# Gate and value of the last eight units by 15 products over three feature blocks, three contraction blocks and two pairs of units

## The chip, the cores and the metric

The kernel runs on one core of one Trainium2 chip. Its time is the device time of one launch in microseconds, as the median of several runs. The engines are named as in the profile: PE is TensorE (PEld its weight loads), DVE is VectorE, ACT is ScalarE, POOL is GpSimd, SP is SyncE, which here only issues transfers. All data are fp32. A written matmul in fp32 appears as two TensorE instructions in the profile.

## The reference

An RWKV-5 attention over 768 tokens, 4 batches and 8 heads of width 48 is followed by a SwiGLU block on its 3072 output rows of width 384:

```python
for t in range(S):
    cur = einsum(u * k[t], v[t])
    y[t] = einsum(r[t], state + cur)
    state = w * state + einsum(k[t], v[t])
x = y as (3072, 384)
g = x @ w_gate                      # 384 x 1536
silu = g * (1.0 / (1.0 + np.exp(-g)))
out = (silu * (x @ w_val)) @ w_out  # 1536 x 384
```

## The kernel before, in words

**Tiling.** A tile of 128 tokens of one batch is a step `i`, 24 in all. Attention handles one step at a time, in chunks: `scores(i)` (key times query, masked into `At`), `outputs(i)` (the step's output, copied by ACT into `xT`, which holds ten steps), `update(i)` (the state `Z`). From step 12 on, keys and queries are turned by block: `scale_k` and `scale_r` on POOL write them into `hats`, `move_blocks` has SP issue 16 small copies of 32x32 blocks, and `turn_blocks` on DVE transposes within the blocks. A diagonal (`diagonal`, eight ACT operations) is written into `At` before `scores` adds the rest by a predicated copy.

The SwiGLU block works on units `g` of two steps, 256 tokens; there are 12. Width 384 is three contraction blocks of 128 (`CC`), the 1536 features are 12 blocks `f`. `wg` and `wv` hold the gate and value weights, `wo` the output weights. The hidden values of unit `g` are `hT[g]`, twelve blocks of 128 features by 256 tokens.

- Units 0 and 1: `gate_value(g, f)` makes six products per block and unit.
- Units 2 to 11 go in pairs (`four_units(g)` for g = 2, 4, 6, 8, 10). For each feature block the two pairs of operands (gate and value weights; units g and g+1) are multiplied with a seven-product scheme over two contraction blocks, and four plain products add the third: 11 products of 128x256 in place of 12. `w_sums` (POOL) makes sums of weights for two feature blocks at a time, `x_sums` (DVE) sums of inputs for a pair, and after each product ACT or DVE collects the accumulators `c_a` and `c_b` into `hT`. SiLU is a sigmoid on ACT (`sg`) and a product on DVE; the second unit's last product (`h1`) is on POOL.
- `project(g, n)`, n = 0 to 6, makes the output rows of a unit with seven groups of six products of 192 columns, with sums of hidden values from `h_sums` (DVE, tiles `hs`). `two_projections(g)` lists the 14 items of two units in the order "00 10 01 02 11 04 03 12 05 06 13 14 15 16" (unit, n), and hangs `h_sums`, `w_sums` and `x_sums` of the next pair on some of them.

**Order.** All engines run their instructions in the order written. A loop over `s` interleaves attention with SwiGLU work from the list `todo`: `gaps(s, n)` calls `feed`, which takes the next pieces; `queue(g)` puts a pair's pieces on the list when its units exist, and from s = 9 on each group of four steps shares them out evenly. After the loop, `feed(len(todo))` issues what is left and the last two units are projected. In `queue`, the first item of a pair's projections (`then`) is put ahead of the last piece of its `four_units`, and three pieces of the next `four_units` are put between the last items of a projection.

**Memory.** PSUM has four banks for attention (`ps_a`), one each in `ps_w` and `ps_o`, and two in `ps_f`. In SBUF, `hT` is a pool of two buffers, `w_bits` a ring of three (raw weights at first, then `s` and `hs`), `part` a ring of six, `w_low` of two.

Of the kernel before, what the change touches and what calls it, by code (L numbers as in the profile page):

```python
# [9 lines left out]
FP32 = mybir.dt.float32  # L10
INT32 = mybir.dt.int32
UINT32 = mybir.dt.uint32
AF = mybir.ActivationFunctionType
ALU = mybir.AluOpType
AX = mybir.AxisListType
P = 128
# [6 lines left out]
def fast(  # L23
# [25 lines left out]
    B, H, S, D = r.shape  # L49
    D2 = 2 * D  # L50
    VW = 2 * D + 16
    HP = H // 2
    R2 = 64 + D
    NCH = S // P
    N = B * NCH
    DM, DFF = moe_w_gate.shape
    CC, FC = DM // P, DFF // P
# [21 lines left out]
    ones = cst.tile([P, 1], FP32, name="ones")  # L79
    ident = cst.tile([P, P], FP32, name="ident")  # L80
    mask = cst.tile([P, P], FP32, name="mask")
    wg = cst.tile([P, CC, DFF], FP32, name="wg")
    wv = cst.tile([P, CC, DFF], FP32, name="wv")
    wo = cst.tile([P, FC, DM], FP32, name="wo")
    NX = 10
    xT = cst.tile([P, NX, CC, P], FP32, name="xT")
    Z = [cst.tile([P, HP, D2], FP32, name=f"Z{b}") for b in range(B)]
    r_ld = [cst.tile([P, H, D], FP32, name=f"r_ld{i}") for i in range(2)]
    k_ld = [cst.tile([P, H, D], FP32, name=f"k_ld{i}") for i in range(2)]
# [48 lines left out]
    NW = len(chunks)  # L138
# [131 lines left out]
        base=0, pattern=[[1, P]], channel_multiplier=-1,  # L270
    )
    dve.tensor_scalar(held[:], wcol[:], W_LOW, W_HIGH, ALU.max, ALU.min)
    tables = two.tile([P, 2, HP, P + 32], FP32, name="tables", tag="hT")
    pw, pv = tables[:, 0, :, 0 : P + 1], tables[:, 1, :, 0:P]
    dve.memset(pw[:, :, P : P + 1], 1.0)
    dve.tensor_copy(pw[:, :, P - 1 : P], held[:].unsqueeze(2))
    for l in range(7):
        n = 1 << l
# [158 lines left out]
                pool.tensor_mul(ze, ze, w)  # L437


    hT = {}  # L440

    def gate_value(g, f):
        if f == 0:
            hT[g] = two.tile([P, FC, 2 * P], FP32, name="hT", tag="hT")
        gv = ps_f.tile([P, 2, 2 * P], FP32, name="gv", tag="gv")
        for o, wt in enumerate((wg, wv)):
            for c in range(CC):
                pe.matmul(  # L448
                    gv[:, o, :].rearrange("p (i t) -> p i t", i=2),
                    wt[:, c, P * f : P * (f + 1)], xT[:, 2 * g % NX : 2 * g % NX + 2, c, :],  # L450
                    start=(c == 0), stop=(c == CC - 1),
                )
        sg = three.tile([P, 2 * P], FP32, name="sg", tag="sg")
        act.activation(sg[:], gv[:, 0, :], AF.Sigmoid)
        dve.tensor_mul(sg[:], sg[:], gv[:, 0, :])
        dve.tensor_mul(hT[g][:, f, :], sg[:], gv[:, 1, :])
# [101 lines left out]
    def x_halves(g):  # L558

        i = [2 * (g + j) % NX for j in range(2)]  # L560
        return [[xT[:, i[j] : i[j] + 2, c, :] for j in range(2)] for c in range(CC)]

    def x_sums(g):
        (x11, x12), (x21, x22), _ = x_halves(g)
        ta, tb = (two.tile([P, 2, 2, P], FP32, name=n, tag="w_low") for n in ("t12", "t34"))
        t1, t2, t3, t4 = ta[:, 0], ta[:, 1], tb[:, 0], tb[:, 1]
        dve.tensor_sub(t1, x12, x11)
        dve.tensor_sub(t2, x22, t1)
        dve.tensor_sub(t3, x22, x12)
        dve.tensor_sub(t4, x21, t2)  # L570
        part_of.setdefault(g, {})["t"] = (t1, t2, t3, t4)

    def w_sums(g, f):

        (w11, w12, w13), (w21, w22, w23) = (
            [w[:, c, P * f : P * (f + 2)] for c in range(CC)] for w in (wg, wv)
        )
        t = three.tile([P, 4, 2 * P], FP32, name="s", tag="w_bits")
        x = part_of.setdefault(g, {})
        x["s", f] = x["s", f + 1] = t  # L580
        if g == 2:
            pool.tensor_add(t[:, 0], w21, w22)
            pool.tensor_sub(w21, t[:, 0], w11)
        else:
            pool.tensor_add(t[:, 0], w21, w11)  # L585
        pool.tensor_sub(t[:, 1], w22, w21)
        pool.tensor_sub(t[:, 2], w12, w21)
        pool.tensor_sub(t[:, 3], w13, w23)

    def four(g, f, what):  # L590

        x = part_of[g]
        if what == "p1":
            if f == 0:
                for j in range(2):
                    hT[g + j] = two.tile([P, FC, 2 * P], FP32, name="hT", tag="hT")
            x["a", f] = ps_f.tile([P, 2, 2 * P], FP32, name="c_a", tag="gv")[:, 0]
        elif what == "p2":
            pool_of, tag = ((ps_o, "o"), (ps_w, "w_mag"))[f % 2]
            x["b", f] = pool_of.tile([P, 2 * P], FP32, name="c_b", tag=tag)[:]  # L600
        h = [hT[g + j][:, f, :] for j in range(2)]
        if what in ("sg0", "sg1"):
            j = int(what[2])
            x[what, f] = three.tile([P, 2 * P], FP32, name="sg", tag="sg")
            act.activation(x[what, f][:], h[j], AF.Sigmoid)  # L605
            return
        if what == "h1":
            dve.tensor_mul(h[1], h[1], x.pop(("sg1", f))[:])  # L608
            pool.tensor_mul(h[1], h[1], x.pop(("u3", f))[:])  # L609
            return  # L610
        (w11, w12, w13), (s2, w22, w23) = (
            [w[:, c, P * f : P * (f + 1)] for c in range(CC)] for w in (wg, wv)
        )
        (x11, _), (x21, x22), (x31, x32) = x_halves(g)
        s1, s3, s4, s5 = (x["s", f][:, n, P * (f % 2) : P * (f % 2 + 1)] for n in range(4))
        t1, t2, t3, t4 = x["t"]
        acc, lhs, rhs, first = {
            "p1": ("a", w11, x11, True), "p6": ("a", s2, t2, False), "p7": ("a", s3, t3, False),
            "p4": ("a", w22, t4, False), "c21": ("a", w23, x31, False),
            "p2": ("b", w12, x21, True), "c11": ("b", w13, x31, False),  # L620
            "p5": ("b", s1, t1, True), "c22": ("b", w23, x32, False),
            "p3": ("b", s4, x22, False), "c12": ("b", s5, x32, False),
        }[what]
        ps = x[acc, f]
        pe.matmul(  # L625
            ps.rearrange("p (i t) -> p i t", i=2), lhs, rhs,
            start=first, stop=what not in ("p2", "p5", "p4", "p3"), skip_group_check=True,
        )
        if what in ("p1", "p6", "p7"):
            nm = {"p1": "p1", "p6": "u2", "p7": "u3"}[what]  # L630
            x[nm, f] = six.tile([P, 2 * P], FP32, name=nm, tag="part")
            act.copy(x[nm, f][:], ps)  # L632
        elif what == "c11":
            dve.tensor_add(h[0], x.pop(("p1", f))[:], ps)  # L634
        elif what == "c21":
            dve.tensor_mul(h[0], h[0], x.pop(("sg0", f))[:])
            dve.tensor_mul(h[0], h[0], ps)  # L637
        elif what == "c22":
            dve.tensor_add(x["u3", f][:], x["u3", f][:], ps)  # L639
        elif what == "c12":  # L640
            dve.tensor_add(h[1], x.pop(("u2", f))[:], ps)  # L641
# [15 lines left out]
    def two_projections(g):  # L657

        def item(j, p):
            if (j, p) in ((1, 0), (0, 1)):  # L660
                h_sums(g, p)
            elif (j, p) in ((1, 1), (0, 3)):
                h_sums(g + 1, p // 3)
            elif (j, p) == (1, 2) and g + 2 < N // 2:
                w_sums(g + 2, 0)
            elif (j, p) == (0, 6) and g + 2 < N // 2:
                x_sums(g + 2)
            project(g + j, p)
        order = "00 10 01 02 11 04 03 12 05 06 13 14 15 16".split()
        return [lambda j=int(o[0]), p=int(o[1]): item(j, p) for o in order]  # L670


    summed = []
    todo = []
# [9 lines left out]
    def queue(g):  # L684
        if g == 0:
            todo.extend(
                (2 * f2 + 2 if j + f else 0, lambda j=j, f=f: gate_value(j, f))
                for f2 in range(FC // 2) for j in range(2) for f in (2 * f2, 2 * f2 + 1)
            )
        elif g % 2 and g > 1:  # L690
            first, *others = two_projections(g - 3)
            *pieces, last = four_units(g - 1)

            then = two_projections(g - 1)[0]

            for k in range(3):
                others.insert(len(others) - 3 + k, pieces.pop(0))
            pieces = ([first] if g == 3 else []) + others + pieces + [then, last]
            todo.extend((NW + 4, x) for x in pieces)
# [104 lines left out]
    for s in range(4, N + 2):  # L804
# [31 lines left out]
        if s - 2 >= 4:  # L836
            gaps(s, 3)
        gaps(s, 4)
        if s == 12:

            dve.tensor_tensor(bad[:], held[:], wcol[:], ALU.not_equal)
            dve.tensor_reduce(badc[:], bad[:], axis=AX.X, op=ALU.add)
            dve.memset(ones[:], 1.0)
            n_ps = ps_a.tile([P, HP, P], FP32, name="n_ps", tag="a")
            pe.matmul(n_ps[0:1, 0, 0:1], badc[:], ones[:], start=True, stop=True)
            act.copy(outside, n_ps[0:1, 0, 0:1])
    assert done["pool"] == NW
    feed(len(todo))
    for piece in two_projections(N // 2 - 2)[1:]:
        piece()  # L850


# [411 lines left out]
```

## Time and profile before

| what | value |
|---|---|
| runs | 626.18, 625.35, 626.19 us; median 626.18 |
| profiled execution, span of core 0 | 623.3 us, mean granted TensorE clock 0.999 |
| median of the runs less this span | 2.9 us |
| PE busy | 611.0 us, 5040 instructions |
| DVE, ACT, POOL busy | 358.6, 238.9, 296.9 us |
| last product ends | 618.0 us; then an addition of 0.35 us and the output transfer |

The profiled execution's own time is its span and what lies around it on the device; no total is listed for it, so sums are made against the span, and the 2.9 us stand for the rest. In the rows, a line such as L625 is a line of the kernel, followed by engine, operation, output and inputs, shapes and count; after the bar come busy time, mean of one and the idle time before. Matmuls overlap, so their mean is longer than the step from one to the next. Times within the trace count from the start of the span. L625 is the product of `four`, L519 that of `project`, L605 and L608 the sigmoid and product of SiLU, L585 to L588 `w_sums`, L302 `scale_r`.

### The profile page before, as it was taken

What the parts mean: (1) busy time and instruction counts of PE and PEld (TensorE: products, weight loads), DVE (VectorE), ACT (ScalarE), POOL (GpSimd) and SP (SyncE); (2) the same over time, 40 slices, a digit from 0 to 9 for tenths busy, and PEclk for the clock granted to TensorE, in tenths of its full rate; (3) what the DMA queues carried; (4) which work ended last, traced back from release to release, by engine and by line L of the source; (5) the groups of instructions that cost most, each with busy time, mean ns of one, the idle gap of its engine ahead of it and who ended that gap; (6) DMA issues with size and microseconds to landing.
All of it is one profiled execution on the core that took longest, in us unless ns stands there. A gap on an engine that the chain in (4) does not pass through costs nothing.

```text
span 623.3 us, 13014 instructions
## 1 busy us (share of the span) xinstructions
PE 611.0 (98%) x5040; PEld 552.1 (89%) x5040; DVE 358.6 (58%) x751; ACT 238.9 (38%) x647; POOL 296.9 (48%) x350
## 2 busy tenths in 40 slices
PE   8799999999999999999999999999999999999996
PEld 7688888899888899888899888899988899988896
DVE  6888997373566574466575355574354463355460
ACT  3368785312444412344331335422243321233310
POOL 4789789935556315364452636341334211443110
PEclk9999999999999999999999999999999999999999
DMA  7989873233232213322223312221000000000001
GB/s 187 218 215 252 260 242 65 50 62 82 57 60 34 40 16 76 65 42 46 44 34 70 78 16 32 31 41 38 26 1 2 2 0 26 26 1 2 1 2 56
DMA packets 138008, 40.47 MB, mean 65 GB/s; under 512 B 128592, under 2 KB 131792, under 8 KB 137936
## 3 DMA queue, kind: packets, MB, share of 16 engines
q1 hardware_dynamic: 134480, 34.82, 26.4%
q10 hardware_dynamic: 3456, 4.72, 2.1%
q8 instruction: 42, 0.69, 0.5%
q14 instruction: 30, 0.25, 0.1%
HBM read 28.51 MB, written 4.72 MB: 53 GB/s over the span
## 4 chain that ended last, share of the span: by engine, by line
PE 90%; POOL 2%; DMA 1%; ACT 1%; DVE 1%; issue 0%; SPq 0%; ACTq 0%; POOLq 0%
PE c_b L625 25%; PE c_a L625 21%; PE o_f L519 13%; PE o_a L519 8%; PE gv L448 7%; PE o_b L519 6%; PE y_ps L409 5%; PE s_ps L379 3%; PE u_ps L424 1%; PE tp L341 1%; DMA r_ld<-in_r_dram 1%; POOL wg L216 1%; POOL wv L216 1%; POOL rk L228 0%; POOL hats L299 0%
## 5 line engine op out<-in xcount | busy, mean ns | idle before, releaser
L609 POOL TENSOR_TENSOR hT<-hT,u 128x256 f32<-128x256 f32 x60 | 47.0, 785 | 148.7 <-DVE hT L608 121.6
L632 ACT COPY u<-c_a 128x256 f32<-128x256 f32 x120 | 44.5, 371 | 85.8 <-PE c_a L625 83.3
L625 PE MATMUL c_a<-t,wv 128*128 128x256 f32 x240 | 72.1, 382 | 0.1
L625 PE MATMUL c_b<-xT,wg 128*128 128x256 f32 x240 | 71.7, 380 | 0.0
L605 ACT ACTIVATE sg<-hT 128x256 f32<-128x256 f32 x120 | 50.0, 416 | 52.5 <-DVE hT L634 33.8
L320 ACT ACTIVATE At<-ident,du 128x128 f32<-128x128 f32 x176 | 62.0, 398 | 16.0 <-DVE o_sb L533 7.2
L625 PE MATMUL c_b<-xT,s 128*128 128x256 f32 x240 | 61.7, 380 | 0.0
L639 DVE TENSOR_TENSOR u<-u,c_b 128x256 f32<-128x256 f32 x60 | 25.1, 419 | 60.5 <-PE c_b L625 55.4
L625 PEld LDWEIGHTS c_a<-t,wv 128*128 128x128 f32 x240 | 45.0, 190 | 6.8 <-ACT u L632 1.2
L625 PEld LDWEIGHTS c_b<-xT,s 128*128 128x128 f32 x240 | 45.3, 190 | 6.5
L625 PEld LDWEIGHTS c_b<-xT,wg 128*128 128x128 f32 x240 | 45.4, 190 | 5.9
L634 DVE TENSOR_TENSOR hT<-p,c_b 128x256 f32<-128x256 f32 x60 | 25.2, 420 | 41.7 <-PE c_b L625 39.1
L585 POOL TENSOR_TENSOR s<-wv,wg 128x256 f32<-128x256 f32 x24 | 17.6, 734 | 65.5 <-PE o_f L519 50.8
L384 DVE COPY_PREDICATED At<-mask,s_ps 128x512 f32<-128x512 int32 x48 | 33.0, 741 | 21.3 <-PE s_ps L379 12.4
L302 POOL TENSOR_TENSOR hats<-r_ld,rscale 128x384 f32<-128x384 f32 x20 | 20.8, 1040 | 35.3 <-DMA hats<-hats 25.2
L448 PE MATMUL gv<-xT,wg 128*128 128x256 f32 x144 | 36.7, 391 | 0.6 <-ACT xT L413 0.6
L637 DVE TENSOR_TENSOR hT<-hT,c_a 128x256 f32<-128x256 f32 x60 | 25.3, 421 | 19.5 <-PE c_a L625 18.3
L641 DVE TENSOR_TENSOR hT<-u,c_b 128x256 f32<-128x256 f32 x60 | 25.2, 421 | 19.4 <-PE c_b L625 19.2
L625 PE MATMUL c_b<-t,s 128*128 128x256 f32 x120 | 36.2, 383 | 0.0
L409 PE MATMUL y_ps<-At,v_ld 128*32 128x128 f32 x768 | 34.9, 273 | 1.3 <-DVE At L384 1.3
L625 PE MATMUL c_b<-xT,wv 128*128 128x256 f32 x120 | 35.9, 381 | 0.0
L625 PE MATMUL c_a<-t,s 128*128 128x256 f32 x120 | 35.8, 380 | 0.0
(135 smaller groups left out, 1384.3 us busy)
## 6 DMA issues: line engine op xcount, KB each, us to landing
hats<-hats SPq DMA_DIRECT2D x192, 32.0 KB, 2.0
w_bits<-in_moe_w_gate_dram SPq DMA_DIRECT2D x6, 768.0 KB, 6.4
v_ld<-in_v_dram SPq DMA_DIRECT2D x48, 96.0 KB, 3.3
w_bits<-in_moe_w_val_dram SPq DMA_DIRECT2D x6, 768.0 KB, 6.3
w_bits<-in_moe_w_out_dram SPq DMA_DIRECT2D x6, 768.0 KB, 6.7
out_dram<-o_sb ACTq DMA_DIRECT2D x24, 192.0 KB, 1.9
k_ld<-in_k_dram SPq DMA_DIRECT2D x20, 192.0 KB, 3.1
r_ld<-in_r_dram SPq DMA_DIRECT2D x20, 192.0 KB, 3.8
```

The lines of the kernel that those rows point to most:

```text
L320: lambda h=h: act.activation(At[i % 2][:, h, :], ident[:], AF.Identity, scale=du[:, h : h + 1])
L384: dve.copy_predicated(At[i % 2][:].rearrange("p (a e) t -> p a e t", e=2)[:, :, e], mask[:].bitcast(INT32).unsqueeze(1).to_broadcast([P, H ...
L409: pe.matmul(ps[32 * q : 32 * q + 32, cc, :], *x, start=start, stop=stop, skip_group_check=True,)
L448: pe.matmul(gv[:, o, :].rearrange("p (i t) -> p i t", i=2), wt[:, c, P * f : P * (f + 1)], xT[:, 2 * g % NX : 2 * g % NX + 2, c, :], start ...
L519: pe.matmul(ps, lhs[:, f, :], rhs[:, f, :], start=(f == 0 and n in (0, 1, 4)), stop=(f == FH - 1), skip_group_check=True,)
L605: act.activation(x[what, f][:], h[j], AF.Sigmoid)
L609: pool.tensor_mul(h[1], h[1], x.pop(("u3", f))[:])
L625: pe.matmul(ps.rearrange("p (i t) -> p i t", i=2), lhs, rhs, start=first, stop=what not in ("p2", "p5", "p4", "p3"), skip_group_check=True,)
L632: act.copy(x[nm, f][:], ps)
L634: dve.tensor_add(h[0], x.pop(("p1", f))[:], ps)
L637: dve.tensor_mul(h[0], h[0], ps)
L641: dve.tensor_add(h[1], x.pop(("u2", f))[:], ps)
```

## The change

Units 0 to 7 keep their schemes. For units 8 to 11 `four_units` is replaced by `three_units(8)` and `three_units(10)`. A pair of units (512 tokens as two halves of 256) is worked through in four bands of three feature blocks. In each band a bilinear scheme of 15 products (r0 to r14) gives the 3 x 3 x 2 block product; each product is two matmuls, one for gate and one for value, into the two halves of one bank, so a band is 15 rounds of two matmuls of 128x256. The rounds go to seven accumulators: `n`, `y`, `l1`, `l5`, `l8` in attention's four banks in turn, `l4` in `ps_o`, `l2` in `ps_w`. Several rounds add to a bank after it was read once. ACT copies and DVE combinations collect them in `c`, six blocks of 128x512, and SiLU follows on operations of 512 columns: ACT, then DVE for two of a band's three feature blocks and POOL for one.

The weight operands: `in_place` (POOL, 24 operations, hung on the projections of units 6 and 7) overwrites three of nine weight blocks of a band for good; `w_forms` (POOL, nine operations a band) makes six more, in the ring or, for the first two bands of units 10 and 11, in memory of attention. `x_forms` (DVE, 11 operations a pair) makes the inputs' combinations. Buffers of attention hold `c`, the copies and the SiLU values: `hats`, `kT`, `At`, and `r_ld`, `k_ld`, `v_ld`, `Z` for operands.

`wg` and `wv` become the halves of one tile `wgv`, `hT` the halves of one tile `hTs`. `w_sums` no longer overwrites `w21` and makes five sums each time. The pieces of units 8 to 11 leave `todo`: after the loop the order is the first pair's bands, the projections of units 8 and 9 (the last two items between the first rounds of the next pair), the second pair's bands, and all items of units 10 and 11.

```diff
-        t = three.tile([P, 4, 2 * P], FP32, name="s", tag="w_bits")
+        t = three.tile([P, 5, 2 * P], FP32, name="s", tag="w_bits")
...
+        pool.tensor_add(t[:, 0], w21, w22)
+        pool.tensor_sub(t[:, 1], t[:, 0], w11)
+        pool.tensor_sub(t[:, 2], w22, t[:, 1])
+        pool.tensor_sub(t[:, 3], w12, t[:, 1])
+        pool.tensor_sub(t[:, 4], w13, w23)
...
+    THREES = 8
+    ROUNDS = (
+        ("r10", "n"), ("r14", "y"), ("r12", "l4"), ("r6", "l5"), ("r13", "n"), ("r2", "y"),
+        ("r9", "l4"), ("r3", "l1"), ("r5", "n"), ("r11", "y"), ("r7", "l5"), ("r1", "l2"),
+        ("r8", "l8"), ("r4", "l1"), ("r0", "l2"),
+    )
...
+    def prepare_threes(g, n):
+        if g == THREES:
+            if n in (0, 2, 4, 6):
+                in_place(n // 2)
+            if n == 7:
+                for do in w_forms(g, 0):
+                    do()
+        else:
+            if n == 10:
+                x_forms(g)
+            if n in (2, 6):
+                for do in w_forms(g, n // 4):
+                    do()
+
+    def three_step(g, t, n):
+
+        what, chain = ROUNDS[27 - n if t == 3 and n > 12 else n]
+        first = n == [c for _, c in ROUNDS].index(chain)
+        if first:
+            pool_of, tag = {"l4": (ps_o, "o"), "l2": (ps_w, "w_mag")}.get(chain, (ps_a, "a"))
+            wide[chain] = pool_of.tile([P, 2, 2 * P], FP32, name=f"c_{chain}", tag=tag)
+        u, v = wide["u", g, t][what], wide["v", g][what]
+        for o in range(2):
+            pe.matmul(
+                wide[chain][:, o].rearrange("p (i t) -> p i t", i=2), u[:, o], v,
+                start=first and o == 0, stop=True, skip_group_check=True,
+            )
...
+        for t in range(4):
+            z = 15 * t
+            for n in range(15):
+                todo.append((z + n, lambda t=t, n=n: three_step(g, t, n)))
+            if ("u", g, t + 1) not in wide and t < 3:
+                forms = w_forms(g, t + 1)
+                todo.append((z + 0.1, forms[0]))
+                todo += [(z + n + 0.2, do) for n, do in enumerate(forms[1:])]
+            later(z + 0.5, act.copy, q10, "n")
+            later(z + 1.5, act.copy, q14, "y")
+            later(z + 2.5, act.copy, r12, "l4")
+            later(z + 3.5, act.copy, r6, "l5")
+            later(z + 4.5, dve.tensor_add, q14, "n", q14)
+            later(z + 5.5, dve.tensor_add, q10, "y", q10)
+            later(z + 6.5, dve.tensor_sub, c[4], q14, "l4")
+            later(z + 8.5, act.copy, x, "n")
+            later(z + 9.5, act.copy, y, "y")
+            later(z + 9.6, pool.tensor_add, r6, y, r6)
+            later(z + 10.4, dve.tensor_add, c[2], y, "l1")
+            later(z + 10.5, dve.tensor_add, c[5], q10, "l5")
+            later(z + 11.5, dve.tensor_add, r12, r12, "l2")
+            later(z + 12.5, dve.tensor_add, c[3], r6, "l8")
+            r4, r0 = (14.5, 13.5) if t == 3 else (13.5, 14.5)
+            later(z + r4, dve.tensor_sub, c[1], "l1", x)
+            later(z + r4 + 0.1, dve.tensor_sub, c[1], c[1], "l8")
+            later(z + r0, dve.tensor_sub, c[2], c[2], "l2")
+            later(z + r0 + 0.1, dve.tensor_sub, c[0], r12, x)
+            silu(z + 10.8, 0, room["c"][:, 2], hTs[:, :, 3 * t + 2], pool, z + 10.9)
+            for n in range(2):
+                if t == 3:
+                    at = z + 13.7 + n
+                    silu(at, 1 - n, room["c"][:, 0:2, n], hTs[:, n, 9:11], (dve, pool)[n], at + 0.1)
+                else:
+                    silu(z + 15.8 + n, 1 - n, room["c"][:, 1 - n], hTs[:, :, 3 * t + 1 - n],
+                         dve, z + 22.3 + n / 4)
...
             first, *others = two_projections(g - 3)
+            if g - 1 >= THREES:
+                if g - 1 == THREES:
+                    todo.extend((NW + 4, x) for x in others)
+                return
...
+        if s == 24:
+            x_forms(THREES)
...
-    for piece in two_projections(N // 2 - 2)[1:]:
+    projections = two_projections(THREES), two_projections(THREES + 2)
...
+    tail = threes[0] + projections[0][:-2]
+    tail += threes[1][0:1] + projections[0][-2:-1] + threes[1][1:2] + projections[0][-1:]
+    tail += threes[1][2:] + projections[1]
+    for piece in tail:
         piece()
```

## The prediction

> **What bounds the kernel now.** I read the page's busy table and its slices first, then the chain that ended last, then one stretch of pure gate-and-value work.
>
> ```profile
> PE 611.0 (98%) x5040; PEld 552.1 (89%) x5040; DVE 358.6 (58%) x751; ACT 238.9 (38%) x647; POOL 296.9 (48%) x350
> ...
> PE   8799999999999999999999999999999999999996
> ...
> PE 90%; POOL 2%; DMA 1%; ACT 1%; DVE 1%; issue 0%; SPq 0%; ACTq 0%; POOLq 0%
> ```
>
> The first line is busy time by engine, the second TensorE in 40 slices, the third the chain of work by engine. TensorE is full from about 50 us to the last product at 618 us, and no other engine has more than a few per cent of the chain. So the time is the number of TensorE instructions times their pace. The mean of one matmul cannot be that pace: its rows say 380 ns, but they overlap. The pace comes from a window in which only gate-and-value products run (columns: busy us of PE, weight loads, DVE, ACT, POOL, each with its count):
>
> ```profile
> 540.00:586.00 46.00, 46.00 (x215) 40.58 (x214) 23.93 (x59) 17.79 (x49) 14.77 (x21) 1.00 0.00 1
> ```
>
> 215 instructions in 46 us are 0.2140 us each. The row of these products counts two instructions per written matmul (c_a<-t,wv: x240 for 5 pairs x 12 blocks x 2 products), so one 128x256 product costs 0.43 us; the timeline steps by 0.431. An output product of 192 columns steps by 0.325 (1.95 us for six). The rows that price the other engines (count, then busy us and mean ns of one, then idle before):
>
> ```profile
> L343 DVE TENSOR_TENSOR kT<-tp,tables 128x512 f32<-128x512 f32 x4 | 2.7, 687 | 1.8 <-PE tp L341 1.8
> ...
> L492 DVE TENSOR_TENSOR hs<-hT 128x768 f32<-128x768 f32 x12 | 11.8, 984 | 0.0
> ...
> L345 ACT COPY kT<-tp 128x512 f32<-128x512 f32 x8 | 4.6, 573 | 0.0
> ...
> L587 POOL TENSOR_TENSOR s<-wg,wv 128x256 f32<-128x256 f32 x30 | 22.1, 735 | 0.0
> ...
> L302 POOL TENSOR_TENSOR hats<-r_ld,rscale 128x384 f32<-128x384 f32 x20 | 20.8, 1040 | 35.3 <-DMA hats<-hats 25.2 <-DMA v_ld<-in_v_dram 10.0
> ```
>
> The timeline at 408 us has one pair that shows DVE and POOL in each other's way (start, duration, operation):
>
> ```profile
> 408.58 1.00 POOL L302 TENSOR_TENSOR hats<-r_ld,rscale 128x384 f32<-128x384 f32 x1 [10.02 <-DMA v_ld<-in_v_dram]
> ...
> 408.77 1.09 DVE L608 TENSOR_TENSOR hT<-hT,sg 128x256 f32<-128x256 f32 x1
> ```
>
> L608 multiplies two SBUF tensors and takes 0.42 us alone; started 0.19 us after a POOL operation, it took 1.09 and ended 0.3 after it. DVE operations with a PSUM operand stay at 0.42 beside POOL.
>
> **The Trainium skill.** "SBUF — State Buffer", Who interferes with whom: a DVE instruction with two SBUF inputs and a GpSimd instruction that reads SBUF exclude each other, whoever issues first; with at most one SBUF input there is no contention. The L608 pair agrees. "Perfetto Trace Analysis", Identifying the Most-Contended Engine: busy share of matmuls is a poor measure of headroom, weight-load share a better one. Here it is 89%, and the constant 0.431 us step says that the stream has no holes to win, only instructions.
>
> **The change, part by part.**
>
> 1. TensorE work. Units 8 to 11 (two pairs) had 11 products x 12 feature blocks x 2 pairs = 264 written matmuls (`four`). Now each pair has 4 bands of three blocks, 15 rounds, two matmuls a round (gate, value): 240, of the same 128x256 shape. 24 x 0.431 = 10.3 us fewer, all on the path. Nothing else on TensorE changes in number.
>
> 2. The move. `four_units(8)` and (10) stood between the last attention steps and now come after them; these steps keep only the remains of units 6 and 7 and 13 items of their output products (six products each). TensorE loses time only if attention's own loop becomes visible: transposes, 16 copies on SP, transposes again. In the trace the copies for the last step start at 412.33 us, take 10.42 and land 2.0 later (424.8); with 1.4 us of transposes the last scores can run at 426.2. They stand behind (from 391.6 us, where both orders part): 22 products (9.5), one attention step (2.8), 17 products and 18 output products (13.2), step (2.8), 42 output products (13.7): 433.5. So 7 us of cover. The scores before are due at 417 with transposes ready by 412.3. The SP queue order is the same. Cost 0; if the cover went, at most about 3 us.
>
> 3. POOL before the new stage. POOL is stuck in L302 until 408.58, behind SP's transfers, as before; then two `rk` (to 411.8), four `h1` products (2.9), 24 operations of `in_place` (17.6) and nine of `w_forms` (6.6): done at 439. The new stage starts at 433.5 + 2.8 + 24 x 0.325 + 1.7 = 445.8 and wants the first form four rounds later. Covered by 7 us. `x_forms(8)` queues on DVE behind the last output addition (444.7), 11 operations of 0.42; each comes about a round early. Cost 0.
>
> 4. `w_sums` of units 4 to 7 makes five sums, not four: 12 x 0.735 = 8.8 us more POOL, in stages where POOL is idle half the time (L585 alone is preceded by 65 us of idle) and a sum is wanted a block later. The 48 sums of units 8 to 11 (35 us) go. `hTs`, `wgv` only rename memory. Cost 0.
>
> 5. Inside a band (15 x 0.862 = 12.9 us). ACT: 6 copies of 512 at 0.58, 3 sigmoids of 512 at 0.63 (estimate: 0.416 at 256, plus the slope of the copies): 5.4. POOL: 9 forms x 0.735, 3 operations of 512 at 1.30 (estimate from 1.04 at 384 and 2.63 at 1152): 10.5. DVE: 11 combinations and 4 SiLU products of 512, at 0.69 (L343; for SBUF-only between 0.42 at 256 and 0.95 at 768): 10.3, which is 80%, where it was 52%. All fit, so the question is order. I laid a band out by hand, with round n readable at 0.862(n+1)+0.27: every accumulator comes back 0.9 to 1.7 us after its reader is done, but for two. Rounds 13 (due 11.2) and 14 (due 12.1) wait for DVE to read l1 and l2, behind four SiLU products. Those start at 6.9 and end at 9.5 if alone; l1 is then read by 10.2 and l2 by 11.5: 0.6 us in hand. In four bands (the second and third of each pair) POOL is still making forms until about 7.9, and at 9.5 it starts `r6`, 1.3 us long. One lost turn costs DVE 0.6, within the margin; a second, behind `r6`, 1.3: l2 would be read at 13.6 and TensorE lose 1.5. No row shows who wins: 0 to 1.5 each, I take 0.4: +1.6 us. Who waits then: rounds 13 and 14 and all after them.
>
> 6. Band to output products, twice. `four_units` had its last block finished beside an output product. Now the last round ends at E, and DVE and ACT still do c0, a sigmoid, two products, c1, c1, a sigmoid (ACT), two products (POOL), while 18 output products give 5.85 us of cover. `h_sums` wait behind this in DVE's queue; the fourth item (`02`) needs their second sum. Undisturbed it is there at E+6.2: 0.35 lost. With c0 behind POOL's SiLU product and `h_sums` behind POOL's two last ones, E+8.5: 2.7 lost. Between them I take 1.1: +2.2 us. At the end of the kernel nothing more changes: the last addition and the output transfer are the same.
>
> Sum for the profiled execution: 623.3 - 10.3 + 1.6 + 2.2 = 616.8 us of span. The median of the runs, 626.2, is 2.9 above this span, for what lies around it; I carry that over: 619.7 us. Both unknowns at their ends give 616.6 (0 and 0.35 a time) and 627.3 (1.5 and 2.7).
>
> **Rivals.**
>
> - Everything hidden: DVE gets in front of POOL each time. 626.2 - 10.3 = 615.9 or little more. For it: TensorE before shows no bubble with similar chains. Against: DVE at 80% in strict order, and no product left to cover the last band.
> - Attention's loop shows: only output products lie between its steps. Up to 3 us on top of the forecast: 622.7. Against: the 7 us counted above.
> - **Slower: DVE becomes the bound.** Five DVE operations per band have two SBUF inputs, and POOL is 81% busy. If each waits for a POOL operation (0.9, between 0.735 and 1.30), DVE needs 10.3 + 4.5 = 14.8 us per band against 12.9: 1.9 lost in each of 8 bands, 15 us, with the 2.2 of part 6: 633. It turns the sign from 1.0 us per band, (10.3 - 2.2)/8. For it: L608 at 1.09. Against: POOL's work lies mostly where DVE has PSUM operands, and DVE idles about 2 us early in each band, which absorbs part.
> - That the count doesn't fall is excluded by the loops: 15 rounds x 2 x 4 x 2.
>
> **How the numbers follow.** Forecast (617 to 622) 0.54; all hidden 0.22; loop visible 0.12; DVE bound 0.12. The first two and nearly all of the third are faster by over 0.2% (1.25 us, about what a measurement of this kernel can tell from no change): faster 0.83, within 0.2% 0.05, slower 0.12. The range takes in the hidden case and most of the unknowns' upper end: 616.0 to 624.5.
>
> **What would show it.** Right: 240 products of 0.431 in the new stage; TensorE idle of 0.3 to 1.5 us at rounds 13 and 14 in second and third bands, released by DVE's l1 and l2 reads, and before item `02`, released by `hs`; the last attention scores with no wait. Wrong: a steady bubble in all bands, SiLU products of DVE at over 1.3 us each (the slow rival), waits for SP's copies before the last scores, or waits of round 4 for a form.

## The result, and the profile after

| | median, us | runs | profiled span, us |
|---|---|---|---|
| before | 626.19 (625.35 to 626.78) | 5 | 623.3 |
| after | 628.83 (627.92 to 628.9) | 5 | 626.2 |

The ratio is 1.004, with a 95% interval of 1.0028 to 1.0053: the change makes the kernel slower by 2.6 us. The forecast was 619.7, in a range from 616.0 to 624.5; both are wrong, and so is the sign. The granted clock of the profiled execution is 0.997 (before 0.999).

The page of after, in the same three lines as before: busy time by engine, TensorE in 40 slices, the chain of work by engine.

```profile
PE 604.1 (96%) x4992; PEld 541.6 (86%) x4992; DVE 404.1 (65%) x737; ACT 234.7 (37%) x599; POOL 374.3 (60%) x414
...
PE   8799999999999999999999999999999989999986
...
PE 76%; DVE 10%; POOL 4%; issue 1%; SPq 1%; DMA 1%; ACT 1%; DVEq 0%; ACTq 0%; POOLq 0%
```

TensorE has 48 instructions fewer, two for each of the 24 products that went, and is busy 6.9 us less; yet the span grew by 2.9. Slices with an 8 have appeared at the 33rd and the 39th place, where before had a 9. DVE has 14 instructions fewer and is busy 45.5 us **longer**, and it now holds 10% of the chain where it had 1%. So the products were saved, and TensorE now waits for DVE. The waits of TensorE name the work that it waits for (what waited, for which engine's work, us in total, times, the longest):

```profile
PE o_a L520 <- DVE hs L494: 3.7, 2, 1.9
PE c_l L783 <- DVE hats L801: 3.7, 4, 1.1
...
PE c_l L783 <- DVE xf L750: 0.7, 1, 0.7
...
PE c_l L783 <- DVE kT L801: 0.4, 2, 0.2
PE c_a L620 <- ACT p L627: 0.4, 1, 0.4
```

L783 is the product of `three_step`, L801 one of DVE's or POOL's combinations in `later`, L520 the output product, L494 the second sum of `h_sums(g, 0)`, L750 the seventh of the input forms. Not one of these waits was in the trace of before. In time, on TensorE's timeline, for the first of the two pairs (start, duration, operation, and in brackets the idle time before it with what ended it):

```profile
476.18 1.13 PE L783 MATMUL c_l<-xf,wgv 128*128 128x256 f32 x4 [0.70 <-DVE hats L801]
490.86 1.13 PE L783 MATMUL c_l<-xf,wgv 128*128 128x256 f32 x4 [1.13 <-DVE hats L801]
504.62 1.13 PE L783 MATMUL c_l<-r_ld,wgv 128*128 128x256 f32 x4 [0.21 <-DVE kT L801]
514.33 2.19 PE L520 MATMUL o_a<-wt,hs 128*128 128x192 f32 x12 [1.86 <-DVE hs L494]
```

These are the ends of the second, third and fourth band, and the fourth output item `02`. The idle in brackets understates the loss, for the rounds behind it come late as well. Read from start to start, the third band loses 1.73: the two rounds before the wait begin at 487.84, so the next was due 1.72 later at 489.56 and came at 490.86 (1.30 lost); the one after took 1.20 instead of 0.86, the next 0.96. In the same way the second band loses 1.30, the fourth 0.48, the output item 2.03 and 0.1 on the product behind it. All of these come again, within 0.1, in the second pair.

**Why DVE is late in the third band.** DVE's timeline there, and POOL's:

```profile
485.36 0.88 DVE L807 TENSOR_TENSOR At<-At,hats 128x512 f32<-128x512 f32 x1
486.27 1.10 DVE L808 TENSOR_TENSOR hTs<-At,hats 128x512 f32<-128x512 f32 x1
487.30 1.21 DVE L807 TENSOR_TENSOR At<-At,hats 128x512 f32<-128x512 f32 x1
488.54 1.67 DVE L808 TENSOR_TENSOR hTs<-At,hats 128x512 f32<-128x512 f32 x1
490.13 0.67 DVE L801 TENSOR_TENSOR hats<-y,c_l 128x512 f32<-128x512 f32 x1
```

```profile
485.66 1.17 POOL L720 TENSOR_TENSOR s<-s 128x256 f32<-128x256 f32 x1
486.90 1.06 POOL L720 TENSOR_TENSOR s<-s,wgv 128x256 f32<-128x256 f32 x1
487.92 1.74 POOL L801 TENSOR_TENSOR kT<-y,kT 128x512 f32<-128x512 f32 x1
```

The four SiLU products (L807, L808) and POOL's last two weight forms (L720) and `r6` (L801) take turns. Each of the last three DVE products ends 0.55 us after a POOL operation ends, and the fourth, begun while `r6` runs, takes 1.67. Only then does DVE read `l1` (`hats<-y,c_l`) and free the accumulator for round 13. In the fourth band, where POOL makes no forms, the same products of the same shape take

```profile
500.04 0.68 DVE L807 TENSOR_TENSOR At<-At,hats 128x512 f32<-128x512 f32 x1
500.76 0.69 DVE L808 TENSOR_TENSOR hTs<-At,hats 128x512 f32<-128x512 f32 x1
```

**At the start of the stage** the first five input forms on DVE take about twice their time (0.84 to 1.00), while POOL makes the weight forms of the second band; when POOL is through, at 452.3, they fall back to 0.42:

```profile
448.13 1.00 DVE L744 TENSOR_TENSOR xf<-xT 128x256 f32<-128x256 f32 x1
449.05 0.95 DVE L745 TENSOR_TENSOR xf<-xT 128x256 f32<-128x256 f32 x1
...
452.63 0.42 DVE L749 TENSOR_TENSOR xf<-r_ld,xT 128x256 f32<-128x256 f32 x1
```

```profile
448.81 0.91 POOL L720 TENSOR_TENSOR s<-s 128x256 f32<-128x256 f32 x1
449.80 0.79 POOL L720 TENSOR_TENSOR s<-s,wgv 128x256 f32<-128x256 f32 x1
...
451.53 0.79 POOL L720 TENSOR_TENSOR s<-s,wgv 128x256 f32<-128x256 f32 x1
```

**At the change to output products** the two sums that item `02` needs (DVE's timeline) stand beside POOL's two SiLU products of the second unit:

```profile
511.23 0.95 DVE L493 TENSOR_TENSOR hs<-hTs 128x768 f32<-128x768 f32 x1
512.21 1.98 DVE L494 TENSOR_TENSOR hs<-hs,hTs 128x768 f32<-128x768 f32 x1
```

```profile
512.11 1.26 POOL L807 TENSOR_TENSOR At<-At,hats 128x512 f32<-128x512 f32 x1 [4.78 <-ACT At L806]
513.45 1.86 POOL L808 TENSOR_TENSOR hTs<-At,hats 128x512 f32<-128x512 f32 x1
```

L494 began 0.10 us after POOL's first product, waited for it, and took 1.98, where L493 before it took 0.95.

**The account**, from start to start on TensorE:

| place | after, us |
|---|---|
| 24 products of 0.431 | -10.35 |
| first band, input forms | +1.72 |
| second, third, fourth bands, both pairs: 2 x (1.30 + 1.73 + 0.48) | +7.02 |
| change to output products, twice | +4.27 |
| 302 us, the five weight sums | +0.60 |
| first transposes wait longer for their input (no part of the change) | +0.37 |
| sum | +3.6 |

The start of the last product moved by 2.89 (615.87 to 618.76). Some 0.7 us less than this sum was lost. I put it down to steps of about 0.09 at changes from one kind of product to another, of which the new order has fewer; that is not shown, since they were not tried one by one.

### The profile page after: what moved, and what is told of

Its sections match the earlier page's. It is cut to its first block, busy times and chain, and to the rows that moved or that the text cites. A ratio compares the mean times of both kernels' runs of the same rounds, so it can differ in the third digit from the quotient of the medians.

```text
span 626.2 us, 12872 instructions
## 1 busy us (share of the span) xinstructions
PE 604.1 (96%) x4992; PEld 541.6 (86%) x4992; DVE 404.1 (65%) x737; ACT 234.7 (37%) x599; POOL 374.3 (60%) x414
## 4 chain that ended last, share of the span: by engine, by line
PE 76%; DVE 10%; POOL 4%; issue 1%; SPq 1%; DMA 1%; ACT 1%; DVEq 0%; ACTq 0%; POOLq 0%
PE c_b L620 13%; PE o_f L520 12%; PE c_a L620 11%; PE o_a L520 7%; PE gv L449 7%; PE c_l L783 6%; PE o_b L520 6%; PE y_ps L412 5%; PE s_ps L382 3%; DVE hats L801 3%; PE c_n L783 2%; DVE hTs L808 2%; PE c_y L783 2%; DVE At L807 2%; SPq L359 1%
## 5 line engine op out<-in xcount | busy, mean ns | idle before, releaser
L449 PE MATMUL gv<-xT,wgv 128*128 128x256 f32 x288 | 66.8, 385 | 0.6 <-ACT xT L416 0.6
L620 PE MATMUL c_b<-xT,wgv 128*128 128x256 f32 x216 | 64.5, 380 | 0.0
L604 POOL TENSOR_TENSOR hTs<-hTs,u 128x256 f32<-128x256 f32 x36 | 28.7, 799 | 56.4 <-DVE hTs L603 56.2
L449 PEld LDWEIGHTS gv<-xT,wgv 128*128 128x128 f32 x288 | 53.2, 190 | 8.9 <-ACT xT L416 0.9
L620 PEld LDWEIGHTS c_b<-xT,wgv 128*128 128x128 f32 x216 | 40.7, 190 | 5.3
L620 PE MATMUL c_a<-xT,wgv 128*128 128x256 f32 x144 | 42.8, 379 | 0.0
L600 ACT ACTIVATE sg<-hTs 128x256 f32<-128x256 f32 x72 | 29.9, 416 | 30.2 <-DVE hTs L629 21.3
L801 POOL TENSOR_TENSOR kT<-y,kT 128x512 f32<-128x512 f32 x8 | 11.5, 1440 | 38.0 <-ACT y L801 38.0
L412 PEld LDWEIGHTS y_ps<-At,v_ld 128*32 128x32 f32 x768 | 30.3, 110 | 2.4 <-issue 1.4
L620 PEld LDWEIGHTS c_a<-t,s 128*128 128x128 f32 x144 | 26.8, 190 | 4.4 <-ACT p L627 0.8
L620 PEld LDWEIGHTS c_a<-xT,wgv 128*128 128x128 f32 x144 | 27.3, 190 | 3.6
```

The source lines that it names most:

```text
L412: pe.matmul(ps[32 * q : 32 * q + 32, cc, :], *x, start=start, stop=stop, skip_group_check=True,)
L449: pe.matmul(gv[:, o, :].rearrange("p (i t) -> p i t", i=2), wt[:, c, P * f : P * (f + 1)], xT[:, 2 * g % NX : 2 * g % NX + 2, c, :], start ...
L620: pe.matmul(ps.rearrange("p (i t) -> p i t", i=2), lhs, rhs, start=first, stop=what not in ("p2", "p5", "p4", "p3"), skip_group_check=True,)
L801: todo.append((at, lambda: do(out, *(bank(a) if isinstance(a, str) else a for a in args))))
```

## The experiments

Theory: DVE instructions with two SBUF inputs and POOL's instructions take turns, and wherever DVE's results are wanted within a microsecond or two this shows on TensorE. First rival: the new scheme is bound by DVE in any order. Second rival: a repaired wait gives way to another. All ratios below are against the kernel before, run on the same chip as the experiment; its medians there were 625.14 (e1, e2, e4, e5), 625.52 (e6 to e9) and 625.37 (e10).

**e2_silu_early.** The SiLU products of a band's second block are written 3.5 rounds earlier in DVE's queue, so that only two, not four, stand ahead of the reads of `l1` and `l2`:

```diff
-                         dve, z + 22.3 + n / 4)
+                         dve, z + (18.85, 22.55)[n])
```

> In bands 0 to 2 the two SiLU products of a band's second block are put ahead of the first combination of the next band, into the 2.3 us in which DVE idles there; those of the first block stay where they were. Theory (rounds 13 and 14 wait since four SBUF-only products lose turns to POOL in one row): the 1.3 and 1.7 us of the second and third bands go, and most of the 0.5 of the fourth: 6.5 of 13.2 us in all, 622.3. Rival (DVE is full over a whole band, the order does not matter): the wait turns up at round 4 or 8 of the same bands, 628 to 629.

Measured: 621.80 us (621.09 to 624.42), ratio 0.9952 (0.9938 to 0.9967). All waits at rounds 13 and 14 are gone, those of the fourth band too; `hs` (1.88 and 1.87) and the input forms (1.15) are left. These are all the waits of TensorE from 440 us on:

```profile
PE o_a L520 <- DVE hs L494: 3.8, 2, 1.9
PE c_l L783 <- DVE xf L750: 1.2, 1, 1.2
```

The profiled span falls from 626.2 to 619.3, by 6.9, against 7.02 in the account; these are single executions. By the medians, each against the kernel before on its own chip (2.64 above it in after, 3.34 below it here), the gain is 6.0. The products still take 1.08 to 1.22 in the second and third bands: the contention remains, it only no longer stands ahead of a read that TensorE waits for. So the order cost these 6 to 7 us, and DVE does not bind the bands.

**e5_no_forms.** No weight forms are made within the bands; the later bands multiply with the operands of an earlier one. It leaves out that part of the computation, and no other.

```diff
-                forms = w_forms(g, t + 1)
-                todo.append((z + 0.1, forms[0]))
-                todo += [(z + n + 0.2, do) for n, do in enumerate(forms[1:])]
+                todo.append((z + 0.1, lambda t=t: wide.update({("u", g, t + 1): wide["u", g, t]})))
```

> Leaves out the weight forms of all bands but those made before the new stage: later bands use the weights and forms of an earlier one, so POOL makes no forms during the bands; every product, copy, combination and SiLU operation stays. Theory (POOL's forms shut DVE out): the waits of rounds 13 and 14 in the second and third bands go (6.0 us) and the input forms run at 0.42 each (1.5 us): 621.3. Rival (SiLU products stand too late in DVE's queue, POOL or not): only the 1.5 goes, 627.3.

Measured: 620.40 us (620.12 to 620.86), ratio 0.9924 (0.991 to 0.9939). DVE's order is as in after, with all four products ahead of `l1`, and there is no wait in the second and third bands. DVE's timeline at the end of the third band:

```profile
483.08 0.69 DVE L808 TENSOR_TENSOR hTs<-At,hats 128x512 f32<-128x512 f32 x1
483.69 0.68 DVE L807 TENSOR_TENSOR At<-At,hats 128x512 f32<-128x512 f32 x1
484.41 0.69 DVE L808 TENSOR_TENSOR hTs<-At,hats 128x512 f32<-128x512 f32 x1
485.02 0.68 DVE L801 TENSOR_TENSOR hats<-y,c_l 128x512 f32<-128x512 f32 x1
```

Without POOL beside it DVE does the four in 2.7 us, where it took 4.8. The waits for the input forms are gone as well. The waits for `hs` stay at 1.87, as they must: the two SiLU products of POOL are still there. The 0.22 of the fourth band stays too; it is no contention but a shorter wait for `l2` there, since the last band runs round 14 (`r0`) ahead of round 13.

**e1_xforms_early.** The input forms for units 8 and 9 go ahead of attention's last outputs and of the output additions:

```diff
-        if s == 24:
+        if s == 23:
             x_forms(THREES)
```

> x_forms(8) is issued one attention step earlier (after s = 23), nothing else. Theory (the forms of the next band on POOL shut DVE out of its second SBUF read, so the input forms took 0.94 us each where 0.42 was reckoned): the first band of units 8 and 9 loses 1.7 us now and 0.1 then, 628.8 becomes 627.1. Rival (the first band is held by its chain of copies, whatever the inputs): the wait moves to a later round of the same band, 628.8.

Measured: 627.79 us (627.54 to 628.55), ratio 1.0039 (1.0026 to 1.0052), no gain, where one of 1.7 us was expected. The waits for `xf` are gone and one for ACT has come, on TensorE's timeline:

```profile
445.64 2.22 PE L520 MATMUL o_f<-wt,hTs 128*128 128x192 f32 x12 [1.17 <-ACT u L528]
```

Eleven input forms stand ahead of an output addition on DVE. ACT's queue holds that addition's output transfer, and behind it the copy `u` (L528) that frees the bank for the next output product. The second rival is right here: TensorE waits before the stage instead of in its first rounds, behind another engine, and loses about 1.4 us there from start to start, where it lost 1.72.

**e9_xforms_split.** e2, with only the four input forms of the first rounds moved, to just after the last predicated copy of `scores`; the other seven stay.

```diff
             scores(s - 1)
+            if s == 24:
+                x_forms(THREES, 0)
...
         if s == 24:
-            x_forms(THREES)
+            x_forms(THREES, 1)
```

> With the early SiLU products of e2; the first four input forms of units 8 and 9 go right behind the last scores' predicated copy, the other seven stay behind the last output addition. Theory (the first band waits for input forms that stand behind that addition and run at half speed beside POOL): 1.2 to 1.5 us less than e2: 620.5. Rival (as in e1, whatever is put ahead of the output additions holds ACT's output transfer and with it the copy that item 15 waits for): 621.8 or more, with a wait of an output product on ACT.

Measured: 621.33 us (620.26 to 621.91), ratio 0.9927 (0.9914 to 0.994). The profile has neither the wait for `xf` nor one for ACT; `hs` is left with 1.88, twice. The gain over e2 is 0.0025 of the time, 1.6 us, with intervals that overlap, so that it is not certain; 620.5 was expected. The four forms are in time now although three of them still take 0.83 to 0.94.

**e4_all_three.** e2 and e1 together, and the first unit's last SiLU products on DVE only after the last combinations, so that the combinations for POOL's products come first.

```diff
-                    silu(at, 1 - n, room["c"][:, 0:2, n], hTs[:, n, 9:11], (dve, pool)[n], at + 0.1)
+                    silu(at, 1 - n, room["c"][:, 0:2, n], hTs[:, n, 9:11], (dve, pool)[n], z + 14.8)
```

> Input forms one step earlier, the second block's SiLU products earlier, and in the last band of a pair the two combinations of c1 ahead of the SiLU products of the first unit. Theory (three separate places where DVE's strict order holds TensorE): 1.7 + 6.5 + 2.8 us go, 617.8, faster than the kernel before by 8.4. Rival (DVE bound): 626 to 629.

Measured: 622.81 us (621.65 to 623.86), ratio 0.9966 (0.9954 to 0.9979): a miss by 5. The ACT wait of e1 is back (1.18), and `hs` waits 2.09 twice, more than in after. POOL's products came earlier, and now both sums stand beside them: L493 took 1.84 and L494 1.90, and POOL went on to the next pair's forms, beside the sums for the seventh item. To start POOL earlier moved its work onto the sums.

**e8_second_unit_late.** e2, with the second unit's last SiLU products taken from POOL and put on DVE **behind** the first unit's sums; as in e4, the last combinations come ahead of the first unit's products. POOL has nothing of the first pair left to do there.

```diff
+                        def second(sg=sg, gate=gate, value=value):
+                            dve.tensor_mul(sg, sg, gate)
+                            dve.tensor_mul(hTs[:, 1, 9:11], sg, value)
+
+                        wide["late", g] = second
...
+    def with_late(g, items):
+        return items[0:2] + [wide["late", g]] + items[2:]
```

> With the early SiLU products of e2; in the last band of a pair c1 is combined ahead of the first unit's SiLU products, and those of the second unit move from POOL to DVE, behind the first unit's sums of hidden values. Theory (item 02 waits 2.1 us, twice, because the two sums take 1.9 us each beside POOL's two products instead of 1.0, and c1 stands behind a sigmoid): the wait falls to 0.3 at most, 3.6 us less than e2: 618.2 where e2 gave 621.8. Rival (DVE's own chain from the last round is too long for 5.85 us of cover, POOL or not): the wait stays over 1.5, 620.5 to 622.

Measured: 621.85 us (621.34 to 622.6), ratio 0.9941 (0.9928 to 0.9954), 3.7 above what was expected, inside the rival's 620.5 to 622 and no faster than e2. But the timeline of TensorE has the two changes to output products behave differently:

```profile
511.24 2.19 PE L520 MATMUL o_a<-wt,hs 128*128 128x192 f32 x12 [1.64 <-DVE hs L494]
516.48 2.22 PE L520 MATMUL o_f<-wo,hs 128*128 128x192 f32 x12 [1.10 <-DVE o_sb L530]
592.53 2.19 PE L520 MATMUL o_a<-wt,hs 128*128 128x192 f32 x12 [0.27 <-DVE hs L494]
```

The code is the same at both. At the second the wait is 0.27; at the first POOL, with nothing else to do, has started the forms of the next pair, which stand later in the written order. DVE's sums there, and one of POOL's forms beside them:

```profile
508.41 1.29 DVE L493 TENSOR_TENSOR hs<-hTs 128x768 f32<-128x768 f32 x1
509.74 1.36 DVE L494 TENSOR_TENSOR hs<-hs,hTs 128x768 f32<-128x768 f32 x1
```

```profile
508.85 1.44 POOL L720 TENSOR_TENSOR v_ld<-At 128x256 f32<-128x256 f32 x1
```

At the second change both sums take 0.96. The rival, that DVE's own chain is too long with or without POOL, would have the wait stay at both changes; the same code with and without POOL's forms is the cleanest case of the theory.

**e7_all_repairs.** e8 and e9 together.

> e8 and e9 together. Theory: their gains add: 626.2 - 10.3 (products) + 0.6 (fifth sum) + 0.5 (small waits) = 617.0. Rival (the waits have one owner, DVE's total work, and move on): 620 or more.

Measured: 619.92 us (619.74 to 620.8), ratio 0.9912 (0.99 to 0.9925): faster than both kernels, though 2.9 above the expected 617.0, because the wait at the first change is as in e8 (1.65, then 1.10). By its time alone it does not part the theory from its rival (620 or more); e10 does.

**e10_forms_held.** e7, with the sigmoid of the second unit's last blocks in `At[1]`. The forms of the next pair are written to the same memory, so POOL can't begin them before DVE has read it, which is behind the first unit's sums. No instruction is added or removed.

```diff
-                        sg = room["sg"][0].rearrange("p (j t) -> p j t", j=2)
+                        sg = at1[:, 0 : 4 * P].rearrange("p (j t) -> p j t", j=2)
```

> e7 with one buffer moved: the sigmoid of the last band's second unit goes into attention's At[1], in whose memory GpSimd writes the next pair's first four weight forms. GpSimd's forms so have to wait until VectorE has made the second unit's SiLU products, that is until the first unit's sums are done. Theory (VectorE's sums at the first change to output products are long because GpSimd starts the next pair's forms as soon as it is idle): the waits there, 1.65 for hs, 0.26 and 1.10 for the output addition in e7, shrink to about 0.3 as at the second change, where no forms follow; 619.9 goes to 617.5. Rival (the work of GpSimd only moves): the forms then run beside the sums for the tenth item or beside the next pair's input forms, and the wait appears there, 1 to 2 us, or at round 4 of the next pair because a form is late; 619 to 620.5.

Measured: 616.96 us (616.46 to 617.84), ratio 0.9863 (0.9841 to 0.9884). It is 2.96 us below e7. The waits at the first change were 2.75 in e7, and 0.27 is left. DVE's timeline there, and POOL's first form:

```profile
505.20 0.96 DVE L493 TENSOR_TENSOR hs<-hTs 128x768 f32<-128x768 f32 x1
506.19 0.96 DVE L494 TENSOR_TENSOR hs<-hs,hTs 128x768 f32<-128x768 f32 x1
507.07 0.69 DVE L854 TENSOR_TENSOR At<-At,hats 128x512 f32<-128x512 f32 x1
507.79 0.69 DVE L855 TENSOR_TENSOR hTs<-At,hats 128x512 f32<-128x512 f32 x1
```

```profile
508.56 4.17 POOL L720 TENSOR_TENSOR At<-wgv 128x256 f32<-128x256 f32 x3 [6.67 <-DVE hTs L855]
```

Both sums take their own 0.96, and item `02` waits 0.27. POOL is held for 6.67 us, and its forms then meet the sums for later items (L497 took 1.48, the next L493 1.21), but those are wanted later and TensorE waits for none of them, nor for a late form. The rival of this run, that the wait only moves, is not borne out.

**e6_before_five_sums.** The kernel before with the five weight sums of the change in `w_sums`, and nothing else.

```diff
-            pool.tensor_add(t[:, 0], w21, w11)
-        pool.tensor_sub(t[:, 1], w22, w21)
-        pool.tensor_sub(t[:, 2], w12, w21)
-        pool.tensor_sub(t[:, 3], w13, w23)
+        pool.tensor_add(t[:, 0], w21, w22)
+        pool.tensor_sub(t[:, 1], t[:, 0], w11)
+        pool.tensor_sub(t[:, 2], w22, t[:, 1])
+        pool.tensor_sub(t[:, 3], w12, t[:, 1])
+        pool.tensor_sub(t[:, 4], w13, w23)
```

> The kernel before with one edit: w_sums makes five sums and leaves w21 alone, for all five pairs (30 groups; 24 of them one POOL operation longer). Theory (the fifth sum pushes h1 products of POOL past the point at which ACT needs their ring buffer: at 302 us the changed kernel lost 0.6 so): slower than before by 0.6 to 1.5 us. Rival (the 0.6 is chance of one execution): no difference.

Measured: 626.38 us (20 runs) against 625.52 (25 runs), ratio 1.0016 (1.001 to 1.0023): 0.9 us slower, with a wait at 302 us that is in after as well and not in before:

```profile
302.32 0.70 PE L622 MATMUL c_a<-t,s 128*128 128x256 f32 x2 [0.39 <-ACT p L629]
```

The two lines of after at that place, TensorE's and ACT's, tell the way:

```profile
302.31 0.70 PE L620 MATMUL c_a<-t,s 128*128 128x256 f32 x2 [0.37 <-ACT p L627]
```

```profile
301.89 0.37 ACT L627 COPY p<-c_a 128x256 f32<-128x256 f32 x1 [1.76 <-POOL hTs L604]
```

POOL makes a fifth sum ahead of a SiLU product (L604). ACT's copy `p` needs a buffer of the ring `part` that this product still reads, and it comes 1.76 late; TensorE needs the bank that `p` empties.

## Why the prediction was wrong, point by point

The steps that failed: two parts that were put at nothing cost TensorE 1.72 and 0.6 us (points 3 and 4), and two whose mechanism was right were sized at 1.6 and 2.2 us and measured 7.0 and 4.3 (points 5 and 6).

1. **24 products, -10.3: right.** 48 instructions went, and rounds of two products step by 0.862 to 0.864.
2. **Attention's loop covered, 0: right.** No wait stands before the last scores. There is a slip of counting: between two of the steps stand 22 products, not 17. It makes 2.2 of the 3.6 us by which the stage starts later than reckoned (449.4 and not 445.8); it moves cover, not the end.
3. **POOL before the stage and input forms, 0: wrong.** This step failed at "11 operations of 0.42". That is their time alone; the first five ran at 0.84 to 1.00, and 1.72 us were lost. The step has POOL done with the first band's forms before the stage, and does not ask what POOL starts then: it went straight on to the forms of the second band. It also ran late: the forms of the first band ended at 445.2, not 439, since seven of the 24 operations of `in_place` took 1.3 to 1.4 instead of 0.73. On time, at nine forms of 0.73, POOL would have been through the second band's forms by 445.6, ahead of the input forms at 448.1. This last is an estimate from these figures, not tried.
4. **The fifth sum, 0: wrong.** "POOL is idle half the time" is a mean over stages. At one place of 12 a SiLU product was queued behind the sum with 0.4 to 0.5 us too little to spare. It cost 0.6 in after; e6, with the sum in all pairs, was slower by 0.9.
5. **The bands, +1.6: right mechanism, wrong size, 7.0 measured.** The order that the prediction laid out is what happened: forms, then `r6`, and `l1` and `l2` read behind it. But the prediction had POOL pause between them, with the forms done 7.9 us into a band and `r6` at 9.5. In the third band the last form ended 9.6 us after the band's first product (478.35 to 487.96), as forms lost turns too, and `r6` followed at once. I gave DVE one lost turn and part of a second, 0.4 us a band. DVE lost a turn on each of the four products there (on three in the second band), 4.8 us where e5 has 2.7, and TensorE lost 1.73 and 1.30, about the 1.5 that stood at the upper end. A single turn cost less than I had put: 0.2 to 0.5 beside a form and 1.0 beside `r6`, not 0.6 and 1.3; there were more of them. Two streams in order that exclude each other, each with its next instruction ready, alternate in these lines; there was no reason to take the middle. Here the Trainium skill helps: "SBUF — State Buffer", SBUF: two separate sides, says of a DVE instruction with two SBUF inputs and a GpSimd one that whichever starts first has the shared pair of ports for the whole instruction and that the other blocks fully. The trace agrees (L808, 1.67 against 0.69, begun while `r6` ran). The fourth band's 0.48, twice, was not in the sum: with rounds 13 and 14 exchanged, `l2` is wanted one round, 0.86 us, sooner than in the other bands, and the margin of 0.6 was worked out for those.
6. **Band to output products, +2.2: right mechanism, wrong size, 4.3 measured.** 2.1 each lies within the 0.35 to 2.7 of the prediction, nearer its upper end. Two of the three delays of that end came: `c0` stood behind POOL's SiLU product (at 506.40, 1.47 instead of 0.69), and the second sum behind POOL's first product of the second unit (1.98 instead of 0.96). The first sum kept its 0.95. I took a point between two ends although the work of POOL there (ACT's second sigmoid, then two products) starts just when DVE gets to the sums, with nothing in the order to keep them apart.

Of the rivals, **DVE becomes the bound** comes nearest, but is not it. Its SiLU products did take up to 1.67, but lengthened in the four bands with forms only, and the mean over eight bands is 7.0 / 8 = 0.88 us, below the 1.9 that it had and below the 1.0 that it gave for a change of sign. In e10 nothing was taken from DVE (two instructions were even added for each pair), and the kernel is 1.37% faster than before. With the bands alone mis-sized the forecast would have been 626.2 - 10.3 + 7.0 + 2.2 = 625.1. The sign turned by the sum of three: 5.4 more for the bands, 2.1 more at the output products, and 2.3 to 2.6 in two parts that were put at nothing. With the upper ends of both unknowns the prediction itself had 627.3, above its own range.

Where the expected gain went, then: it was all there, and the waits took it. e10 has 8.4 us of the 10.3 (625.37 to 616.96); of the other 1.9 about 0.6 is the fifth sum, as read in after, and 0.5 are two waits of 0.27 for `hs`. Where the rest went is not shown.

## What to carry to other kernels

An instruction of VectorE with two SBUF inputs has no single duration; what it takes depends on what GpSimd has in its queue at that time. Price it by the row only if the timeline shows GpSimd idle there, and otherwise let the two alternate in the sum. In the third band DVE's products of 512 columns ended 1.13 us apart with a form of 256 columns between them and 1.70 us apart with `r6` between them, where they start 0.72 apart alone. A queue can run ahead of its place in the written order: in e8 POOL made forms beside sums that are written before them. "PSUM — Partial Sum Buffer", Engine vs sequencer instructions, calls these queues strict FIFO, which keeps the order within one engine alone; e1 agrees, where ACT's copy `u`, whose product had ended at 442.5, came at 445.28, behind the held output transfer. So when work is taken from GpSimd, ask what it starts instead, and if that is not wanted, give it a buffer that is still in use, as e10 did. And a part that is put at nothing deserves the tightest place looked up, not the mean: here two such parts cost 2.3 to 2.6 us.

## What the runs showed of the hardware

The lengthening goes both ways and reaches some 0.8 of an instruction of the other engine. In after, DVE's instructions with two SBUF inputs go from 0.42 to as much as 1.00 at 256 columns, from 0.69 to 1.67 at 512, and from 0.95 to 2.02 at 768. POOL's go from 0.73 to as much as 1.44 at 256 columns and from 1.28 to 1.86 at 512. Whether an operand comes from PSUM decides it: in after, 58 of DVE's instructions of 512 columns with an input in PSUM ran beside an instruction of POOL, and none took over 0.69; of the 27 with both inputs in SBUF half took 1.10 or more. Two neighbours on DVE's timeline in e10, and POOL's product beside them:

```profile
500.35 0.69 DVE L806 TENSOR_TENSOR hats<-hats,c_l 128x512 f32<-128x512 f32 x1 [0.42 <-PE c_l L788]
500.96 1.48 DVE L806 TENSOR_TENSOR hats<-kT,x 128x512 f32<-128x512 f32 x1
```

```profile
500.62 1.27 POOL L813 TENSOR_TENSOR hTs<-At,hats 128x512 f32<-128x512 f32 x1
```

The first has one input in PSUM (`c_l`) and keeps its 0.69 with POOL busy; the second has both in SBUF and takes 1.48. POOL's own product, which was first, keeps its 1.27.
